# A causal convolution on TensorE: from two column tiles of 64 to four of 32

## The chip, the cores and the metric

The kernel runs on one core of a Trainium2 chip. A core has TensorE (PE: matmuls, and PEld for the weight loads that go with them), VectorE (DVE), ScalarE (ACT), GpSimd (POOL) and SyncE (SP), each with its own stream of instructions, and 16 DMA engines that they share. The metric is the device time of one execution in microseconds; a kernel's time is the median of several runs.

## The reference

The input x has 8 sequences of 3264 rows and 192 channels. A causal convolution of 7 taps comes first, with softmaxed weights of its own for each of 8 heads of 24 channels. Then a spectral mix: the lowest 64 modes of a Fourier transform along the sequence are multiplied by a complex 192 x 192 matrix for each mode, transformed back and added, and a channel matmul with ReLU is added to that.

```python
# convolution: H = 8 heads, K = 7 taps, group = D // H
w = softmax(weight)
out = np.einsum('hk,bskhg->bshg', w, x_unf)     # x_unf: the 7 rows up to s

# spectral mix of x = out
X = np.fft.rfft(x, axis=1)
Yr = einsum('bmd,mde->bme', Xr, w_r) - einsum('bmd,mde->bme', Xi, w_i)
Yi = einsum('bmd,mde->bme', Xr, w_i) + einsum('bmd,mde->bme', Xi, w_r)
Y[:, :n_modes] = Yr + 1j * Yi
y = np.fft.irfft(Y, n=S, axis=1)
u = x + y
return u + np.maximum(u @ w_ch, 0.0)
```

## The kernel before

The eight sequences are taken as four pairs (`q`), and each pair as 13 blocks (`t`) of 256 rows, the last of 192. A block is loaded as two halves of 128 rows, one row to a partition, into `xall`. Blocks are grouped into units: the first pair in four (2, 3, 4 and 4 blocks), the others in three (5, 4, 4), 13 units in all.

There are three stages, written in a fixed order of instructions (`manual_schedule`), which each engine keeps.

**Convolution and DFT.** `conv_group(k, g)` convolves unit `k` for two heads, so a unit has four groups. The convolution is a matmul with a band matrix made from the taps: `band[:, e, h, :]` gives, from 128 input rows, the outputs at even (`e = 0`) or odd (`e = 1`) rows. Output goes to PSUM, where partition p holds rows 2p and 2p + 1 of the block. L309 makes 64 output partitions from each half of 128 rows, on column tile 0 or 64 of the PE array. A few outputs need rows from the half before: L317 adds them for the upper 64 partitions, L314 for the lower ones from the block before, L321 for the first block of a unit, whose rows before are kept in `side` (L336). ACT (L328) or DVE (L330) then copies the group back over `xall`, as bf16, and three PSUM buffers `zc` go round. `dft_unit` (L344) sums the blocks' Fourier transforms with the table `ftab`, which DVE and ACT compute at the start (`table_dve`, `table_act`) from the row numbers `sidx` that a POOL iota made (L164).

**Weights.** PE transposes the table (`g_bank`, L421) and the convolved blocks (`ct_bank`, L431), and between these multiplies the modes by their matrices (`mix`, L471), four modes to a group, 16 groups. The matrices have seven slots; a slot's next load is issued after the mix that read it (`load_free`, L281).

**Output.** For each of 52 blocks 28 matmuls (L501), a ReLU on ACT (L528), an addition on DVE (`finish`, L536) and a store from SP (L540), into buffers that go round.

All loads of x and of the matrices are DMAs issued by POOL in program order. At the start these are units 0 to 3, a memset of the unused half of the last blocks (L252), the last blocks of all pairs (`load_last`, L155), then POOL's own small constants and units 4 on (L143), the small matrices, and the mode matrices (L281). L237 builds the band matrix: 152 matmuls of 8 columns on four column tiles of 32.

## Time and profile before

| what | value |
|---|---|
| median of 3 runs | 184.12 us (183.80 to 184.87) |
| the profiled execution, its own time | 183.47 us |
| its span in the profile | 181.7 us, mean granted PE clock 0.979 |
| instructions of the profile | 7678 |
| PE busy, weight loads busy | 165.1 us (91%), 140.1 us (77%) |
| DVE, ACT, POOL busy | 113.9 us (63%), 99.1 us (55%), 52.2 us (29%) |
| DMA | 40.27 MB moved, mean 222 GB/s |
| stores from SP | 52, one for each block, 372 ns median to issue, 3.7 us to landing |

The profile page has the busy time of each engine, the span in 40 equal slices of 4.54 us (each digit is a share in tenths), the DMA queues, the chain of work that ended last, and the costliest groups of instructions. In the chain a piece is a start, a length and what ran; "issue" is time in which the engine waited for nothing that the profile shows. In a timeline a row is a start, a length, engine, line, operation, output and inputs, and in brackets the idle time before it and what ended it. L-numbers are lines of the kernel.

### The profile page before, as it was taken

To read this page: it belongs to the slowest core of one execution; us is meant where nothing else is said; L and a number is where in the kernel's file an instruction comes from. 1 tells how busy PE (TensorE), PEld (TensorE's weight loads), DVE (VectorE), ACT (ScalarE), POOL (GpSimd) and SP (SyncE) were. 2 spreads that over 40 slices of the span, in tenths; PEclk is the share of its full clock that TensorE was granted. 3 is DMA by queue.
4 is the path that set the end of the run, shared out by engine and by line. 5 is a ranking of instruction groups with operands and counts; after the bars stand their busy time and mean duration, and the time that the engine had idled before them with its cause. 6 is when DMAs were issued, how large, how long until landed. Compare 5 with 4: busy or idle time off the path is not lost.

```text
span 181.7 us, 7678 instructions
## 1 busy us (share of the span) xinstructions
PE 165.1 (91%) x3440; PEld 140.1 (77%) x3440; DVE 113.9 (63%) x160; ACT 99.1 (55%) x138; POOL 52.2 (29%) x84
## 2 busy tenths in 40 slices
PE   7958799999999997999999985899999999999970
PEld 2437578888887885788997852499999999999960
DVE  3676944444544554577767600678888888888880
ACT  2442593353362452568777721666666666666750
POOL 7995694434322744055520220000000000000000
PEclk9996999999999999999999999999999999999995
DMA  2999999999999999999999394069998999999995
GB/s 24 159 166 190 191 192 195 189 193 192 191 192 193 205 206 207 206 192 190 201 207 207 59 174 79 4 236 338 345 316 318 361 330 349 341 323 330 351 352 171
DMA packets 49808, 40.27 MB, mean 222 GB/s; under 512 B 28399, under 2 KB 49775, under 8 KB 49775
## 3 DMA queue, kind: packets, MB, share of 16 engines
q0 software_dynamic: 35680, 19.69, 79.0%
q1 hardware_dynamic: 14095, 20.09, 31.5%
q8 instruction: 27, 0.44, 0.9%
q14 instruction: 6, 0.05, 0.1%
HBM read 39.40 MB, written 20.05 MB: 327 GB/s over the span
## 4 chain that ended last, share of the span: by engine, by line
PE 80%; DMA 6%; ACT 4%; issue 3%; DVE 3%; POOL 0%; DVEq 0%; ACTq 0%
PE z_right L501 17%; PE z_left L501 16%; PE w_left L431 10%; PE x_right L344 9%; PE x_left L309 8%; DMA arena<-in_moe_w_i_dram 4%; PE x_right L309 3%; PE w_right L471 3%; PE x_left L317 3%; PE x_left L314 2%; DMA ct<-in_weight_dram 2%; PE w_left L421 2%; PE x_right L317 2%; PE x_right L189 1%; ACT xall L328 1%
## 5 line engine op out<-in xcount | busy, mean ns | idle before, releaser
L501 PEld LDWEIGHTS <-gt 64*128 64x128 bf16 (+1 forms) x832 | 35.9, 96 | 1.7 <-issue 1.6
L309 PEld LDWEIGHTS <-bandyet 128*64 128x64 bf16 x416 | 32.2, 114 | 4.9 <-issue 4.1
L317 PE MATMUL x_left<-xall,bandyet 128*64 128x192 bf16 (+3 forms) x140 | 26.5, 254 | 3.9 <-issue 3.9
L330 DVE CAST xall<-x_left 128x768 bf16<-128x768 f32 (+3 forms) x18 | 16.8, 935 | 20.5 <-PE x_left L321 10.8
L309 PE MATMUL x_left<-xall,bandyet 128*64 128x192 bf16 (+3 forms) x280 | 27.9, 256 | 0.2 <-ACT xall L328 0.2
L501 PEld LDWEIGHTS <-ct 64*128 64x128 bf16 (+1 forms) x624 | 27.3, 96 | 0.5 <-issue 0.4
L143 POOL DMA_DIRECT2D xall<-in_x_dram x26 | 22.9, 884 | 14.9 <-DMA xall<-in_x_dram 13.8
L317 PEld LDWEIGHTS <-bandyet 128*64 128x64 bf16 x208 | 23.5, 114 | 4.3 <-issue 4.3
L314 PE MATMUL x_left<-xall,bandyet 128*64 128x144 bf16 (+3 forms) x140 | 25.8, 232 | 0.0
L528 ACT ACTIVATE z_right<-z_right 128x768 f32<-128x768 f32 (+1 forms) x26 | 20.7, 794 | 9.4 <-PE z_right L501 9.0
L528 ACT ACTIVATE z_left<-z_left 128x768 f32<-128x768 f32 (+1 forms) x26 | 20.7, 795 | 9.0 <-PE z_left L501 9.0
L501 PE MATMUL z_left<-fz,gt 64*128 64x192 bf16 (+1 forms) x416 | 24.7, 243 | 0.1
L501 PE MATMUL z_right<-fz,gt 64*128 64x192 bf16 (+1 forms) x416 | 24.2, 243 | 0.5 <-ACT z_right L528 0.5
L314 PEld LDWEIGHTS <-bandyet 128*64 128x64 bf16 x208 | 23.6, 116 | 0.0
L328 ACT CAST xall<-x_left 128x768 bf16<-128x768 f32 (+3 forms) x17 | 13.9, 816 | 14.5 <-DVE side L336 7.4
L409 DVE COPY ct<-w_left 128x1024 bf16<-128x1024 bf16 x24 | 15.9, 689 | 7.4 <-PE w_left L431 5.3
L344 PE MATMUL x_right<-xall,fz 128*128 128x384 bf16 (+1 forms) x104 | 19.2, 327 | 1.4 <-DVE xall L330 1.1
L431 PE MATMUL w_left<-ident,xall 128*128 128x128 bf16 x312 | 19.6, 220 | 0.0
L431 PEld LDWEIGHTS <-xall 128*128 128x128 bf16 x312 | 17.6, 103 | 1.8 <-issue 0.3
L501 PE MATMUL z_right<-wch,ct 64*128 64x192 bf16 (+1 forms) x312 | 17.5, 243 | 0.2 <-ACT fz L448 0.2
L501 PE MATMUL z_left<-wch,ct 64*128 64x192 bf16 (+1 forms) x312 | 17.5, 243 | 0.0
L407 ACT COPY ct<-w_left 128x1024 bf16<-128x1024 bf16 (+1 forms) x16 | 15.3, 960 | 3.7 <-PE w_left L431 3.4
(109 smaller groups left out, 292.0 us busy)
## 6 DMA issues: line engine op xcount, KB each, us to landing
out_dram<-arena SPq DMA_DIRECT2D x25, 384.0 KB, 3.7
out_dram<-xt SPq DMA_DIRECT2D x12, 384.0 KB, 3.8
out_dram<-ct SPq DMA_DIRECT2D x11, 384.0 KB, 3.5
xall<-in_x_dram POOLq DMA_DIRECT2D x8, 384.0 KB, 14.0
xall<-in_x_dram POOLq DMA_DIRECT2D x10, 288.0 KB, 12.8
xall<-in_x_dram POOLq DMA_DIRECT2D x6, 480.0 KB, 14.4
ct<-in_moe_w_r_dram POOLq DMA_DIRECT2D x8, 288.0 KB, 7.8
ct<-in_moe_w_i_dram POOLq DMA_DIRECT2D x8, 288.0 KB, 8.3
```

What stands on the lines that cost most here:

```text
L143: nc.gpsimd.dma_start(out=dst, in_=src)
L309: nc.tensor.matmul(cols[r, :, e, :].rearrange("p t (i d) -> p t i d", i=2), band[:, e, h, 0:64], xall[:, q, t0:t0 + n, half, :, dsl], star ...
L314: nc.tensor.matmul(cols[0:64, 1:n, e, :].rearrange("p t (i d) -> p t i d", i=2), band[:, e, h, 64:P], xall[:, q, t0:t0 + n - 1, 1, :, dsl] ...
L317: nc.tensor.matmul(cols[64:P, :, e, :].rearrange("p t (i d) -> p t i d", i=2), band[:, e, h, 64:P], xall[:, q, t0:t0 + n, 0, :, dsl], star ...
L328: nc.scalar.copy(out=dst, in_=srcv)
L330: nc.vector.tensor_copy(out=dst, in_=srcv)
L344: nc.tensor.matmul(xp, ftab[0:r, 2 * t + e, :], xall[0:r, q, t, e, :, :].rearrange("p i d -> p (i d)"), start=(t == 0 and e == 0), stop=(t ...
L407: nc.scalar.copy(out=out, in_=in_)
L409: nc.vector.tensor_copy(out=out, in_=in_)
L431: nc.tensor.transpose(tp[:, P * k:P * k + P], src, ident[:])
L501: nc.tensor.matmul(zt[0:l.shape[-1], i, D * e:D * e + D], l, r, start=begin, stop=end, tile_position=(64 * i, 0), skip_group_check=True)
L528: nc.scalar.activation(out=zt[0:m, :, 0:2 * D], in_=zt[0:m, :, 0:2 * D], func=ACT.Relu)
```

## The change

Three things are changed.

The convolution makes 32 output partitions at a time, on column tiles 0, 32, 64 and 96 (`tile_position=(0, 32 * ct_)`). Only the first 32 of each 64 outputs of a half need rows from the half before, so the matmuls for these ("spill") go to two of the four tiles. Even blocks (`t`) stand as before; odd blocks are stored 32 partitions on, so that their spill goes to the other two tiles. Even and odd blocks are separate matmuls, with every second block of the unit in the columns.

The row numbers in `sidx` follow the rotation, with three iotas, and a finished odd block is stored in two transfers: partitions 32 to 127, and partitions 0 to 31, which hold its last 64 rows.

On POOL's queue the memset of the unused half goes between the loads of the second and third unit, and the loads of the last blocks go ahead of those of the fourth.

```diff
-    nc.gpsimd.iota(sidx.rearrange("p (t e) -> p t e", e=2), pattern=[[256, NB], [1, 2]], base=0,
-                   channel_multiplier=2, allow_small_or_imprecise_dtypes=True)
+    s3 = sidx.rearrange("p (t e) -> p t e", e=2)
+    for t0, p0, p1, base in ((0, 0, P, 0), (1, 0, P, 256 - 64), (1, 0, 32, 256 + 192)):
+        nc.gpsimd.iota(s3[p0:p1, t0:NB:2, :], pattern=[[512, (NB + 1 - t0) // 2], [1, 2]], base=base,
+                       channel_multiplier=2, allow_small_or_imprecise_dtypes=True)
...
     load_unit(*units[1])
+    nc.gpsimd.memset(xall[64:P, :, NB - 1, 1, :, :], 0.0)
     load_unit(*units[2])
+    load_last(0)
+    load_last(1)
     load_unit(*units[3])
...
-    nc.gpsimd.memset(xall[64:P, :, NB - 1, 1, :, :], 0.0)
-    load_last(0)
-    load_last(1)
...
-        for hd in range(2):
+        def mm(hd, e, c, spill, odd):
             h = 2 * g + hd
             dsl = slice(GRP * h, GRP * h + GRP)
-            cols = zt[:, hd, 0:96 * n].rearrange("p (t e c) -> p t e c", t=n, e=2)
...
+            ct_ = (c + odd) % 4
+            t1 = t0 + (t0 + odd) % 2
+            out = zt[32 * ct_:32 * ct_ + 32, hd, 0:96 * n].rearrange("p (t e c) -> p t e c", t=n, e=2)
+            lhs = band[:, e, h, 64:96] if spill else band[:, e, h, 32 * (c % 2):32 * (c % 2) + 32]
+            first = e == 0 and odd == t0 % 2 and not spill
+            def one(ts, src):
+                o = out[:, ts[0] - t0:ts[-1] + 1 - t0:2, e, :].rearrange("p t (i d) -> p t i d", i=2)
+                nc.tensor.matmul(o, lhs, src, start=first, stop=False, tile_position=(0, 32 * ct_),
+                                 skip_group_check=True)
+            ts = list(range(t1, t0 + n, 2))
+            if spill and c == 0:
+                back = [t for t in ts if t > t0]
+                if back:
+                    one(back, xall[:, q, back[0] - 1:back[-1]:2, 1, :, dsl])
+                if ts[0] == t0 and t0:
+                    one(ts[:1], sd[:, :, dsl].unsqueeze(1))
+            else:
+                one(ts, xall[:, q, ts[0]:ts[-1] + 1:2, (c - spill) // 2, :, dsl])
+        w = t0 % 2
+        for hd in range(2):
             for e in range(2):
-                for half in range(2):
...
+                for c in range(4):
+                    mm(hd, e, c, 0, w)
+                mm(hd, e, 0, 1, w)
+                mm(hd, e, 2, 1, w)
+                for c, spill in ((0, 0), (2, 0), (0, 1), (2, 1), (1, 0), (3, 0)):
+                    mm(hd, e, c, spill, 1 - w)
...
-        dst = bass.AP(tensor=out.tensor, offset=out.offset + (2 * q * S + 256 * t) * D,
-                      ap=[[2 * D, m], [S * D, 2], [1, 2 * D]])
-        nc.sync.dma_start(out=dst, in_=o[0:m].rearrange("p i e d -> p i (e d)"))
+        for p0, p1, r0 in (((32, P, 0), (0, 32, 192)) if t % 2 else ((0, m, 0),)):
+            dst = bass.AP(tensor=out.tensor, offset=out.offset + (2 * q * S + 256 * t + r0) * D,
+                          ap=[[2 * D, p1 - p0], [S * D, 2], [1, 2 * D]])
+            nc.sync.dma_start(out=dst, in_=o[p0:p1].rearrange("p i e d -> p i (e d)"))
```

More of the change, by code (lines that the diff above doesn't have):

```diff
@@ L301, in conv_group @@
         sd = side[k % 2]
-        for hd in range(2):
+        def mm(hd, e, c, spill, odd):
             h = 2 * g + hd
             dsl = slice(GRP * h, GRP * h + GRP)
-            cols = zt[:, hd, 0:96 * n].rearrange("p (t e c) -> p t e c", t=n, e=2)
-            for e in range(2):
-                for half in range(2):
-                    r = slice(64 * half, 64 * half + 64)
-                    nc.tensor.matmul(cols[r, :, e, :].rearrange("p t (i d) -> p t i d", i=2),
-                                     band[:, e, h, 0:64], xall[:, q, t0:t0 + n, half, :, dsl],
-                                     start=(e == 0), stop=False, tile_position=(0, 64 * half),
-                                     skip_group_check=True)
-                if n > 1:
-                    nc.tensor.matmul(cols[0:64, 1:n, e, :].rearrange("p t (i d) -> p t i d", i=2),
-                                     band[:, e, h, 64:P], xall[:, q, t0:t0 + n - 1, 1, :, dsl],
-                                     start=False, stop=False, tile_position=(0, 0), skip_group_check=True)
-                nc.tensor.matmul(cols[64:P, :, e, :].rearrange("p t (i d) -> p t i d", i=2),
-                                 band[:, e, h, 64:P], xall[:, q, t0:t0 + n, 0, :, dsl],
-                                 start=False, stop=(t0 == 0), tile_position=(0, 64), skip_group_check=True)
-                if t0:
-                    nc.tensor.matmul(cols[0:64, 0, e, :].rearrange("p (i d) -> p i d", i=2),
-                                     band[:, e, h, 64:P], sd[:, :, dsl],
-                                     start=False, stop=True, tile_position=(0, 0), skip_group_check=True)
```

## The prediction

> **What bounds the kernel now.** I read the slices first, then the chain of waits, then the PE's timeline inside the convolution, and last the DMA queue that carries instructions.

> ```profile
> PE   7958799999999997999999985899999999999970
> PEclk9996999999999999999999999999999999999995
> DMA  2999999999999999999999394069998999999995
> ...
> q8 instruction: 27, 0.44, 0.9%
> ```

> The DMA engines are full from slice 1 on (4.5 us) to about 100 us, and the PE from slice 5 (about 23 us) on. The chain says which ends last:

> ```profile
> 71.45 0.97 DVE xall L330
> 72.46 1.48 PE x_right L344 x8
> 73.94 1.01 PE w_left L421 x32
> ...
> 104.79 0.60 POOL arena L281
> 105.39 6.60 DMA arena<-in_moe_w_i_dram
> 112.03 0.48 PE w_right L471 x12
> ```

> Convolution and DFT are a PE chain up to 73.9 us. The weight stage is a PE chain of 30.2 us up to the mix that frees the last slot (104.1), then a 6.6 us load. The output stage is PE again, 1.155 us a block. So a shift of the 73.9 moves the end one for one, until the loads themselves come last. The x loads (10.0 MB at 192 GB/s) are done near 58 us, the seven weight groups that have a free slot (4.1 MB at 206 GB/s) near 78.

> The PE's timeline holds the line that decides this case:

> ```profile
> 6.29 1.38 PE L237 MATMUL x_right<-ct 7*32 7x8 bf16 x152 [0.22 <-DVE ct L233]
> ...
> 11.29 0.19 PE L314 MATMUL x_left<-xall,bandyet 128*64 128x48 bf16 x1
> 14.30 0.29 PE L317 MATMUL x_left<-xall,bandyet 128*64 128x96 bf16 x1 [2.81 <-issue]
> ...
> 19.62 0.23 PE L314 MATMUL x_left<-xall,bandyet 128*64 128x144 bf16 x1
> 20.97 0.27 PE L317 MATMUL x_left<-xall,bandyet 128*64 128x192 bf16 x1 [1.12 <-issue]
> ```

> Twice the PE stops inside a conv group, between an L314 and an L317 that read data which is already there; "issue" means that the profile shows nothing it waited for. From 14.30 to the second stop, one window counts:

> ```profile
> 14.30:20.96 6.66, 5.37 (x127) 5.10 (x127) 5.71 (x8) 2.53 (x4) 3.63 (x5) 0.78 1.60 191
> 28.66:35.18 6.52, 6.52 (x135) 5.63 (x131) 3.34 (x4) 3.20 (x4) 3.31 (x4) 1.00 1.60 192
> 42.41:48.92 6.51, 6.51 (x133) 5.62 (x129) 3.10 (x4) 3.20 (x4) 2.74 (x4) 1.00 1.60 192
> ```

> **Matmuls (conv_group).** A group of four blocks now has five matmuls per head and parity, 768 columns in sum on two column tiles of 64: 4 x 768 / 2 columns; it takes 0.69 us (41.77 to 42.46). After the change it has 12 matmuls per head and parity, mostly of 96 columns, 13 where history comes from the side buffer: 4 x 1152 / 4, three quarters of the columns, if four tiles overlap as two do now: 0.52 us. Seven eighths of the convolution lies behind 26 us: 45 of 52 blocks, at 8.8 us per 13 blocks (four groups of 0.82, eight of 0.69), 30.5 us, of which a quarter is 7.6 us. That is the whole gain.

> No row shows 128 rows by 32 columns with 96 moving columns. Nearest is L237: 152 pairs on four tiles of 32 in 1.38 us, 9.1 ns a pair, here 10 ns from the columns. The other bound is that only two of four overlap: 20 ns, 1.04 us a group. I take 10 ns; both lie under the fetch, below.

> [...]

> **Instructions.** The order of instructions of the two programs has 976 conv matmuls before and 2,624 after, each with its weight load: 3,296 instructions more. Up to the first transpose of the weight stage (L421 now) it counts 2,569 before and 5,865 after. The stall at 14.30 is at row 446 of that order; it stays where it is, as the page asked for at 6.9 us does. Behind it stand (5865 - 446) / 255 = 21.2 pages (255: a semaphore wait each) instead of 8.3. A page's work is 128 pairs at 10 ns plus its share of the DFT (8 matmuls of 0.175 us to about 1.9 pages), some 2.1 us: less than any fetch above. So the PE starves:
> - 14.3 to 27.0 us: 2 pages (6.6, 6.1).
> - 27.0 to 58, x loads running: 31 / 5.15 = 6.0 pages.
> - 58 to 78, weight loads running: 20 / 4.75 = 4.2 pages.
> - then no data moves, since group 7 waits for the first mix: 9.0 pages x 2.9 = 26.1 us, to 104.1.
> - the last copy and DFT, 1.5 us of the 2.5 that the chain shows: 105.6.

> The weight stage starts at 105.6 instead of 73.9, 31.7 us later, and keeps its 38.1 us: its PE work asks for a page every 6.6 us, its loads again wait for the mixes. Sum on the profiled execution: 183.5 + 31.7 = 215.2 us. That run is 0.65 under the median of 184.12, inside the spread of the runs; I say 215.

> Bounds: pages of 4.4 us while data moves and 2.3 idle (no 0.5 of the tail, which both stalls have under load) give 11.6 + 2 pages by 78, 7.6 x 2.3 = 17.5, end near 97, 207 us. Pages of 5.5, and 3.9 idle (the slowest of the output stage) give 9.3 + 2, 9.9 x 3.9, end near 118, 228. A stalled PE also loses clock (0.60 in the window 14 to 18 us, after the first stall): at half clock a page's 2.1 us become 4.2, hidden under load, up to 1.3 a page over 2.9 without, 12 us at most.

> [...]

> **The rest is nothing, and what covers it.** Two more iotas (0.31 us each now) and the memset of 1.37 us go ahead of the third unit's loads on POOL; the loads issued by then are 0.96 MB, 5 to 6 us at 160 GB/s, which covers these 2 us. Without that cover x would come 2 us later, under a PE that is late anyway. The four DMAs of the last blocks (2.98 us of POOL) pass the two of the fourth unit: the same bytes in another order, for a unit that the PE reaches after 27 us. The iotas feed L200 at 6.16 us and end before 4. On SP, 24 blocks get a second store: an issue is 0.37 us, so 0.74 in a period of 1.155, no queue; uncovered it would be 24 x 0.37 = 9 us. Bytes and rows are the same; the last block keeps one transfer. DVE and ACT run as many instructions as before.

> **Rivals.**
> 1. Faster, 176 us: fetching keeps up and four tiles overlap. The 7.6 us come off; the last loads allow about that much (after 78 us, nine groups of 2.9 us end at 104.4 instead of 112.0). For it: 220 instructions per us ran at L237, and the burst needed no wait. Against: that burst came from what was loaded at the start, and the stall followed it. It decides if a page takes under 2.9 us while data moves. 7%.
> 2. Slower by little, 187 us: every page takes the 2.9 us that row 102.9 shows, the long ones being only late requests. 14.3 + 21.2 x 2.9 + 1.5 = 77.3, 3.4 us later. Against: 6.66 us between two stalls is no late request. 8%.
> 3. The fetch binds as above and the pair costs 20 ns or the clock halves in the idle stretch: 9 pages x 1.3 more, 227 us. 12%.
> That it does not do what it says: the order of instructions shows the 2,624 matmuls, so this falls away.

> **How the numbers follow.** Forecast 215 at 73%. The range reaches down to 200, between the second rival and the low bound of 207, and up to 226, just short of the third. About 0.5% is what a measurement of this kernel can tell from no change: faster 0.07, within it 0.01, slower 0.92.

> **What would show it.** The PE's waits name "issue" some twenty times, 2 to 5 us each in units of 256 instructions; q8 moves 40 packets, 0.65 MB; the first transpose starts near 105 us; the DMA row shows a hole between 78 and 105; PEclk falls below 9 in the convolution; a block of the output stage stays at 1.155 us. If q8's packets come less than 2.5 us apart while x loads run, my reading of one page at a time is wrong, and with it the forecast; if the convolution's pairs take over 40 ns without waits named "issue", the PE and not the fetch was the bound.

## The result, and the profile after

| what | before | after |
|---|---|---|
| median of 4 runs | 184.19 us (183.80 to 184.87) | 242.69 us (241.94 to 245.00) |
| the profiled execution's span | 181.7 us | 240.2 us |
| first transpose of the weight stage starts | 73.94 us | 122.07 us |
| last addition of the output stage starts | 176.48 us | 226.77 us |
| from there to the end of the span | 5.2 us | 13.4 us |

The change makes the kernel slower: ratio 1.319, 95% interval 1.309 to 1.330. The forecast was 215 us with a range of 200 to 226, so the direction was right and the size was not.

The span grew by 58.5 us, and three rows of the table say where: 48.1 us up to the first transpose, 2.2 us more up to the last addition (50.3 - 48.1), and 8.2 us behind it. The page after shows the first and the last of these in its slices of 6.0 us:

```profile
PE   7523365585564866969599999868999999999600
PEclk9955557587796799997979999999999999999975
DMA  5999999999999200000006999480899899899985
...
q8 instruction: 40, 0.66, 1.0%
```

Counted from 0, slices 1 to 19 show a PE that is busy about half of most of them. DMA stands nearly still from slice 14 to slice 20 (84 to 126 us), waiting for the first mix, and in the last two slices stores run while the PE has nothing left. The instruction queue moved 40 packets, as forecast. The chain of waits (start, length, what ran) shows what filled the first part:

```profile
12.96 0.47 PE x_left L318 x20
13.51 0.48 PE x_right L318 x26
13.99 0.60 PE x_left L318 x31
14.59 4.93 issue
19.52 0.84 PE x_left L318 x34
...
119.38 0.97 DVE xall L346
120.39 1.68 PE x_right L360 x8
122.07 1.85 PE w_left L437 x16
...
154.90 6.24 DMA arena<-in_moe_w_i_dram
...
226.77 0.95 DVE arena L552
```

A burst of convolution matmuls from 12.96 us, 1.63 us long, then 4.93 us in which nothing that the profile shows was waited for. The engine's waits, summed over 9 to 119 us (us in total, times, longest), name nothing else of that size on the PE. The two rows are largely the same stalls, seen by the weight loads and by the matmuls, and are not to be added:

```profile
PEld L318 <- issue: 50.4, 33, 5.1
...
PE x_left L318 <- issue: 35.9, 16, 4.9
```

The windows from one page boundary to the next (stretch, length, busy time and count of PE, weight loads, DVE, ACT, POOL, then granted clock, DMA share, GB/s) give the price of a page of 256 instructions:

```profile
12.96:19.53 6.57, 1.64 (x129) 1.50 (x129) 3.15 (x5) 1.22 (x2) 5.89 (x11) 0.50 1.59 191
25.72:32.07 6.35, 2.35 (x128) 2.13 (x128) 2.15 (x3) 3.12 (x4) 2.26 (x4) 0.50 1.60 192
50.84:57.04 6.20, 3.38 (x129) 2.44 (x129) 1.57 (x3) 1.44 (x2) 1.76 (x3) 0.97 1.60 192
88.56:92.29 3.73, 3.46 (x128) 2.45 (x128) 0.96 (x1) 1.32 (x2) 0.00 (x0) 1.00 0.02 4
99.31:103.13 3.82, 3.37 (x128) 2.40 (x128) 2.37 (x3) 1.44 (x2) 0.00 (x0) 1.00 0.02 4
```

A page is some 128 pairs of a weight load and its matmul. While x is loaded (192 GB/s) a page takes 6.1 to 6.6 us, whatever the PE's own part is, 1.64 or 3.38 us; beside the matrix loads after that it takes 5.9 to 6.0. With the data queues still it takes 3.4 to 3.9, but for one page (107.04 to 111.70 us) in which the PE itself was busy throughout, at a granted clock of 0.63. Eleven pages from 12.96 to 81.10 us take 6.19 us on average, the nine from 84.93 to 118.86 take 3.77. The queue itself shows one such page under load and one in the idle stretch, with the windows 50.84 to 57.04 and 99.31 to 103.13 cut into 40 slices of 155 and 95 ns:

```profile
GB/s 196 191 193 193 191 191 191 186 188 191 193 196 198 193 188 188 193 191 188 188 193 186 198 196 294 186 176 176 181 173 178 186 188 191 193 196 196 186 188 186
...
q8 instruction: 1, 0.02, 1.0%
...
GB/s 0 0 0 0 0 0 0 0 0 0 0 172 0 0 0 0 0 0 0 0 0 0 0 0 0 0 0 0 0 0 0 0 0 0 0 0 0 0 0 0
...
q8 instruction: 1, 0.02, 1.9%
```

In the idle page the packet starts 1.1 us after the page ahead was entered (slice 11; a packet's bytes are put down at its start). It takes 1.2 us (1.9% of 16 engines' 3.82 us), and the PE goes on 1.5 us after it ended. Under load (slice 24 of the first row) the same three parts are 3.9, 0.95 and 1.4 us: nearly the whole difference between 6.2 and 3.8 is the time until the packet starts.

### The profile page after: what moved, and what is told of

Read it like the earlier page. It is cut to its first block, busy times and chain, and to the rows that moved or that the text cites. A ratio compares the mean times of both kernels' runs of the same rounds, so it can differ in the third digit from the quotient of the medians.

```text
span 240.2 us, 11017 instructions
## 1 busy us (share of the span) xinstructions
PE 175.7 (73%) x5086; PEld 143.5 (60%) x5088; DVE 112.9 (47%) x160; ACT 99.6 (41%) x138; POOL 52.9 (22%) x86
## 4 chain that ended last, share of the span: by engine, by line
PE 64%; issue 18%; DMA 6%; DVE 4%; ACT 2%; SPq 0%; POOL 0%; DVEq 0%; ACTq 0%
PE x_left L318 12%; PE z_right L517 12%; PE x_right L360 10%; PE z_left L517 10%; PE w_left L447 8%; PE x_right L318 5%; DMA arena<-in_moe_w_i_dram 3%; PE w_right L487 2%; DMA out_dram<-arena 2%; PE w_left L437 2%; DMA ct<-in_weight_dram 2%; DVE arena L552 1%; PE w_right L500 1%; PE x_right L373 1%; PE w_left L455 1%
## 5 line engine op out<-in xcount | busy, mean ns | idle before, releaser
L318 PEld LDWEIGHTS <-bandyet 128*32 128x32 bf16 x2624 | 37.5, 108 | 52.2 <-issue 50.4
L318 PE MATMUL x_left<-xall,bandyet 128*32 128x96 bf16 (+2 forms) x1668 | 32.1, 228 | 32.1 <-issue 31.4
L344 ACT CAST xall<-x_left 128x768 bf16<-128x768 f32 (+3 forms) x17 | 13.9, 818 | 42.5 <-PE x_left L318 33.4
L360 PE MATMUL x_right<-xall,fz 128*128 128x384 bf16 (+1 forms) x104 | 25.6, 404 | 1.1 <-DVE xall L346 1.1
L344 ACT CAST xall<-x_right 128x768 bf16<-128x768 f32 (+1 forms) x9 | 6.9, 764 | 35.4 <-PE x_right L318 31.3
L318 PE MATMUL x_right<-xall,bandyet 128*32 128x96 bf16 (+2 forms) x812 | 16.0, 226 | 4.9 <-issue 4.9
L318 PE MATMUL x_left<-side,bandyet 128*32 128x48 bf16 x92 | 16.2, 197 | 4.5 <-issue 4.5
L284 POOL DMA_DIRECT2D ct<-in_moe_w_r_dram x8 | 5.0, 619 | 61.4 <-PE w_right L487 59.0
L346 DVE CAST xall<-x_right 128x768 bf16<-128x768 f32 (+2 forms) x8 | 8.1, 1008 | 21.5 <-PE x_right L318 21.3
L517 PE MATMUL z_left<-wch,ct 64*128 64x192 bf16 (+1 forms) x312 | 17.5, 243 | 0.0
```

Of the source, the lines that this page charges most:

```text
L284: nc.gpsimd.dma_start(out=slots[slot_of[g]][64 * half:64 * half + 64, :, :, :], in_=src[4 * g:4 * g + 4, :, :].rearrange("m (p j) e -> p m ...
L318: nc.tensor.matmul(o, lhs, src, start=first, stop=False, tile_position=(0, 32 * ct_), skip_group_check=True)
L344: nc.scalar.copy(out=dst, in_=srcv)
L346: nc.vector.tensor_copy(out=dst, in_=srcv)
L360: nc.tensor.matmul(xp, ftab[0:r, 2 * t + e, :], xall[0:r, q, t, e, :, :].rearrange("p i d -> p (i d)"), start=(t == 0 and e == 0), stop=(t ...
L517: nc.tensor.matmul(zt[0:l.shape[-1], i, D * e:D * e + D], l, r, start=begin, stop=end, tile_position=(64 * i, 0), skip_group_check=True)
```

## The experiments

**The stores, put back alone.** The changed kernel with one store for each block:

```diff
-        for p0, p1, r0 in (((32, P, 0), (0, 32, 192)) if t % 2 else ((0, m, 0),)):
...
+        dst = bass.AP(tensor=out.tensor, offset=out.offset + (2 * q * S + 256 * t) * D,
+                      ap=[[2 * D, m], [S * D, 2], [1, 2 * D]])
+        nc.sync.dma_start(out=dst, in_=o[0:m].rearrange("p i e d -> p i (e d)"))
```

> The changed kernel with one store for an odd block: the rows of odd blocks land rotated by 64 rows in the output, the bytes are the same. If the second store makes the output stage longer, as the 13 us between the last addition and the end suggest, the whole is near 233 us and that gap is back at 5 us. If the stores are not the cause, 242 us.

Measured 231.98 us, ratio 1.255 (1.237 to 1.274). The first transpose starts at 120.53 and the span is 229.4 us, 47.7 over before: without the second stores the kernel is late by the convolution and by little else. The medians differ by 10.7 us. But the profiles put 1.5 us of that ahead of the first transpose (122.07 against 120.53), where nothing is stored yet. From the start of the last addition to the end it is 5.8 us here, and 13.4 with the second stores. So the second stores are worth some 8 to 9 us: a term of the forecast that stood at nothing is about a seventh of the loss.

**The stores, added alone to the kernel before.** Odd blocks of the old kernel stored in two, cut in three ways: partitions 32 to 127 and 0 to 31 as in the change, two halves of 64 partitions, or all 128 partitions with one sequence each.

```diff
+        for p0, p1 in (((32, P), (0, 32)) if t % 2 else ((0, m),)):      # split
+        for p0, p1 in (((64, P), (0, 64)) if t % 2 else ((0, m),)):      # split64
+        for i0, i1 in (((0, 1), (1, 2)) if t % 2 else ((0, 2),)):        # splitseq
...
```

> The kernel before, with odd blocks stored in two transfers of 96 and 32 partitions, in place (no rotation). If the split alone makes the output stage longer: about 9 us more, 193 us. If it is hidden, as predicted: 184 us.

> The kernel before, with odd blocks stored in two transfers of all 128 partitions, one for each sequence: as many transfers as in the split by partitions. Theory that the number of transfers costs: the same 193 us. Theory that transfers of few partitions cost: 184 to 186 us.

> The kernel before, with odd blocks stored in two transfers of 64 partitions. Number of transfers: 193 us as for 96 and 32. Few partitions: between 184 and 193 us, or more than 193 if every transfer under 128 partitions is slow.

Measured: split 192.38 us, ratio 1.045 (1.038 to 1.052); split64 192.78, 1.048 (1.041 to 1.055); splitseq 184.34, 1.001 (0.997 to 1.005). All three issue 76 transfers instead of 52, of the same bytes in sum. So the number of transfers, and with it SP's 24 more issues, costs nothing that shows; a transfer over part of the partitions does. One window of 50 us in the output stage, of split and then of splitseq:

```profile
125.00:175.00 50.00, 49.34 (x1191) 48.87 (x1187) 39.99 (x43) 33.70 (x43) 0.00 (x0) 1.00 0.93 290
```

```profile
125.00:175.00 50.00, 50.00 (x1218) 50.00 (x1214) 41.46 (x44) 34.50 (x44) 0.00 (x0) 1.00 0.95 333
```

The DMA engines are as busy in both (0.93 and 0.95), but move 290 instead of 333 GB/s; before it was 338. The packets of the data are of 1,536 bytes in all of them, and in this window the slowest tenth take 112 ns or more in split, and 73 or more in splitseq and before. An issue on SP has a median of 616 ns in split, 388 in splitseq, 372 before. Whether the longer issues cost time of their own, or only wait for engines that are full, was not tried apart. In the changed kernel SP is behind from the middle of the stage on:

```profile
184.68 2.86 SPq L557 DMA_DIRECT2D out_dram<-arena  x3
187.62 2.73 SPq L557 DMA_DIRECT2D out_dram<-xt  x3
190.44 5.13 SPq L557 DMA_DIRECT2D out_dram<-arena  x6
```

Twelve issues, all but back to back, 0.86 to 0.95 us each on average in a row. The forecast had two of 0.37 us in a period of 1.155.

**When the matrices are loaded.** The changed kernel with the matrix loads held behind the last convolved block, by a small POOL copy that reads it. It tells whether the long page is bound to data moving.

```diff
     dft_unit(len(units) - 1)
+    nc.gpsimd.tensor_copy(out=ct[0:32, 3, 0:16], in_=xall[0:32, NQ - 1, NB - 1, 0, 0, D - 16:D])
     load_free(0)
```

> The changed kernel with the mode matrices' loads held back until the convolution is done, so that no data moves after the x loads end near 58 us. Theory that data traffic makes a page 6.2 instead of 3.6 us: 14 pages at 3.6 us from 58 us on, first transpose near 111 us instead of 122, then the matrices late, the whole near 240 us. Rival (a page's time has nothing to do with the data): first transpose at 122 us and the whole near 252 us.

Measured 244.06 us, ratio 1.321 (1.300 to 1.342). Two windows between page boundaries, one before the x loads end and one after:

```profile
43.98:56.48 12.50, 9.29 (x256) 6.13 (x256) 3.33 (x4) 2.24 (x3) 2.92 (x5) 0.75 1.60 192
70.96:107.37 36.41, 27.11 (x1278) 20.29 (x1277) 14.24 (x18) 11.97 (x16) 0.00 (x0) 1.00 0.02 5
```

Two pages take 12.5 us under load, 6.25 each; the ten from 70.96 us on take 36.41, 3.64 each, of which the PE is busy 2.71. The changed kernel was still at 6.0 a page there (69.17 to 75.18 to 81.10) in the same part of the program. So the loads set the longer price. The last copy of the convolution is done by 112.6, 7.7 us earlier than the changed kernel's at 120.35, and the matrices, now loaded behind it, take that back.

**Only the number of instructions, first attempt.** The kernel before, with 8 or 4 more tiny matmuls for each head and parity, into columns of PSUM that nobody reads (`shift`, 7 x 32, as in L237):

```diff
             for e in range(2):
+                for x in range(8):                                       # pad4: range(4)
+                    nc.tensor.matmul(xtrb[32 * (x % 4):32 * (x % 4) + 32, 500:508], shift[0:KK, 0:32], taps_t[0:KK, :],
+                                     start=True, stop=True, tile_position=(0, 32 * (x % 4)), skip_group_check=True)
                 for half in range(2):
```

> The kernel before with 1,664 more matmuls of 7 rows, 32 columns and 8 moving columns in the convolution, into columns that nobody reads: 5,897 PE instructions up to the first transpose, as many as in the changed kernel (5,865), with the old column tiles, the old columns and the old single stores. Fetch theory (a page of 256 instructions at a time, 6.2 us while loads run, 3.6 us after): the first transpose near 122 us, as in the changed kernel, the whole near 233 us. Rival (the matmuls themselves, or the narrow tiles, cost the time): 1,664 x 9.1 ns = 15 us, the whole near 199 us.

> The same with 832 more matmuls, 4,233 instructions up to the first transpose, 14.9 pages after the first stall. Fetch theory: 10.6 pages of 6.2 us up to 80, 4.3 of 3.6 us, first transpose near 97 us, the whole near 207 us. Rival: 832 x 9.1 ns = 7.6 us, the whole near 192 us.

Both missed: 269.53 and 271.11 us for 1,664 and 832 more matmuls, or 267.4 and 267.7 in the faster run of each (185.28 before). Half the additions cost the same, so this measured something else than a count. The PE's timeline of the kernel with eight, and the windows of two rounds:

```profile
40.41 0.22 PE L308 MATMUL x_right<-ct 7*32 7x8 bf16 x8
40.56 0.37 PE L312 MATMUL x_right<-xall,bandyet 128*64 128x192 bf16 x2
40.72 0.33 PE L317 MATMUL x_right<-xall,bandyet 128*64 128x144 bf16 x1
...
41.02 0.22 PE L308 MATMUL x_right<-ct 7*32 7x8 bf16 x8
...
40.41:41.02 0.61, 0.61 (x16) 0.47 (x14) 0.00 (x0) 0.61 (x2) 0.61 (x1) 0.50 1.61 193
143.22:143.64 0.42, 0.42 (x16) 0.33 (x13) 0.00 (x0) 0.00 (x0) 0.00 (x0) 1.00 0.00 0
```

A round of 13 matmuls takes 0.61 us (40.41 to 41.02) at a granted clock of 0.50, and 0.42 at 1.00; with four pads it takes 0.58 and 0.40. Before, five took 0.17 at 1.00 (the group of four rounds in 0.69). So part of the loss is a lower clock, 0.83 on average with eight pads and 0.78 with four, and part is there at full clock. The pads alternate small weights on four tiles with large ones on two; whether the tile's width, its rows or the order is to blame was not tried apart. This pair says nothing for or against the fetch, and the pads had to be of the old form.

**Only the number of instructions, in the old form.** Pads with the convolution's own weights and column tiles of 64, 8 columns wide. In pad8w they read `xall`; in pad8x and pad4x (4 instead of 8) the zeros of `blank`, which nothing writes in that stage.

```diff
             for e in range(2):
+                for x in range(8):
+                    p0 = 64 * (x % 2)
+                    nc.tensor.matmul(xtrb[p0:p0 + 64, 500:508], band[:, e, h, 0:64], blank[:, 0:8],
+                                     start=True, stop=True, tile_position=(0, p0), skip_group_check=True)
```

> As pad8, but the 1,664 added matmuls have the shape of the convolution's own: 128 rows, 64 columns on tile 0 or 64, 8 moving columns, so that the array keeps one division. 5,898 instructions up to the first transpose. Fetch theory: pages of 6.2 us until the loads pause near 80 us, then 3.6 to 4, first transpose 119 to 125 us, the whole 230 to 236 us, with waits named issue at every 256 instructions. Rival (what pad8 and pad4 showed is a cost of any added matmul, whatever its shape): as pad8, 269 us, and no such waits.

> As pad8w, but the added matmuls read zeros that nothing overwrites, so that they wait for no copy. Fetch theory: pages of 6.2 us up to about 82 us (row 3,521), then 9.4 pages of 3.6 to 4.0 us (the PE's own work is 3.9), first transpose near 121 us, the whole near 231 us. Rival (the added matmuls' own 16 ns each, as pad8w shows it in the stretch without stalls): 1,664 x 16 ns = 26 us, the whole near 210 us.

> As pad8x with 832 added matmuls, 4,234 instructions up to the first transpose. Fetch theory: 11 pages of 6.2 us to 82 us, then 3.9 pages of 4.3 us (the PE's own work), first transpose near 100 us, the whole near 210 us. Rival: 832 x 16 ns = 13 us, the whole near 197 us.

Measured: pad8w 254.47 us, ratio 1.388 (1.366 to 1.409); pad8x 244.15, 1.328 (1.318 to 1.338); pad4x 216.66, 1.179 (1.170 to 1.188). In pad8w the pads read columns that ACT overwrites, so they wait for copies (0.89 us for `ACT xall L332` before the pads at 95.30 us), a fault of the experiment. Pad8x is the clean one. Its total of 5,897 instructions before the first transpose is that of the changed kernel (5,865) within 0.6%, with the old tiles and stores:

```profile
19.85:26.15 6.30, 4.05 (x128) 3.96 (x127) 4.43 (x6) 1.28 (x2) 5.23 (x8) 0.57 1.60 192
```

A page is 6.30 us here as well. It enters its pages at 13.66, 19.85, 26.15 ... 74.98 and 81.17 us; the changed kernel does at 12.96, 19.53, 25.72 ... 75.18 and 81.10. Twelve boundaries agree within 0.7 us in two programs that share the count and not the tiles. That shows the fetch as the bound while the loads run. Behind 82 us pad8x goes its own way: 4.9 us a page (ten from 81.17 to 130.39 us), with waits of the pads (L309) for the DVE and ACT copies out of `xtrb`, the tile that the pads write (rows of the whole run),

```profile
PE x_right L309 <- issue: 10.1, 6, 2.3
PE x_right L309 <- DVE xt L369: 4.8, 3, 1.6
PE x_right L309 <- ACT xt L371: 3.3, 3, 1.1
```

so its 244 us, 13 over what the fetch theory gave, must not be read as the fetch's price for the whole; the first 80 us are. Pad4x keeps 6.2 us up to 82 us too, is limited by the PE behind it, and ends 7 us over the theory's 210.

**Four tiles without the rotation.** Four column tiles of 32, even and odd blocks in one matmul and one store each: 1,392 convolution matmuls instead of 976 or 2,624. The spill then lies on two tiles only. `one` is a matmul of 32 output partitions on tile 32 * c.

```diff
+                for c in range(4):
+                    one(c, e, False, 0, n, xall[:, q, t0:t0 + n, c // 2, :, dsl])
                 if n > 1:
...
+                    one(0, e, True, 1, n, xall[:, q, t0:t0 + n - 1, 1, :, dsl])
...
+                one(2, e, True, 0, n, xall[:, q, t0:t0 + n, 0, :, dsl])
                 if t0:
...
+                    one(0, e, True, 0, 1, sd[:, :, dsl].unsqueeze(1))
```

> The convolution on four column tiles of 32 without the rotation: even and odd blocks in one matmul of up to 240 columns, spill on tiles 0 and 64, one store for each block. 1,392 conv matmuls, 3,401 instructions up to the first transpose, 11.6 pages after the first stall. Fetch theory: 6.2 us a page up to 80 us, the last page 5.2 (its own work), first transpose near 86 us, the whole near 196 us. Rival (each narrow matmul costs what it cost in the changed kernel, 108 us / 2,624 = 41 ns): 1,392 x 41 ns = 57 us, convolution done near 67 us, the whole near 178 us.

Measured 198.88 us, ratio 1.084 (1.072 to 1.097). Its pages are entered every 5.9 to 6.5 us from 14.83 to 77.08. From its 3,401 instructions and 6.2 us a page, the fetch theory gave 196 before the run; a price of 41 ns for each narrow matmul, the rival, gave 178.

| kernel | instructions to first transpose | first transpose |
|---|---|---|
| before | 2,569 | 73.94 us |
| norot | 3,401 | 88.07 us |
| pad4x | 4,233 | 105.67 us |
| after | 5,865 | 122.07 us |
| pad8x | 5,897 | 134.02 us |

**Fewer instructions and a shorter weight stage.** If instructions are scarce, fewer should help: lean makes the band matrix with 38 matmuls instead of 152. Fill holds ten transposes of the weight stage back for the stretch in which the PE waits for the last matrices; filllean does both.

```diff
-        for g in range(4):
-            nc.tensor.matmul(xtrb[32 * g:32 * g + 32, H * i:H * i + H],
...
+        nc.tensor.matmul(xtrb[0:32, H * i:H * i + H],
...
```

> The kernel before, with the band matrix made by 38 matmuls instead of 152: 228 PE instructions less, all ahead of the first stall. Fetch theory: the two stalls of 2.8 and 1.1 us move and shrink, the convolution ends 1 to 3 us earlier, 181 to 183 us. Rival (the first 26 us are set by the table on DVE and ACT): 184 us.

> The kernel before, with the ten transposes of the last pair (5.6 us of PE) held back until after the mixes: mix 11 and 12 come earlier, so the last two groups of matrices are asked for near 97 us instead of 103, and the transposes fill the wait. Theory that the weight stage ends with the loads: they end near 105 us instead of 112, the whole near 178 us. Rival (the loads come no sooner, or the mixes then wait for their matrices): 184 us.

> fill and lean together. If lean's 1 us at the end of the convolution is worth anything behind fill: 177 us; if the loads are then the bound: as fill.

Lean: 183.23 us, ratio 0.996 (0.992 to 1.001), not told from no change. The two stalls at page boundaries are gone (the first boundary is now crossed at 17.42 us without a wait) and the first transpose comes at 72.88 instead of 73.94, but the PE then waits for x instead. Fill: 185.29, 1.011 (1.001 to 1.021); filllean: 185.83, 1.014 (1.005 to 1.023), both missed the 177 to 178 expected. Fill's chain shows why:

```profile
91.62 11.17 DMA arena<-in_moe_w_i_dram
...
104.41 4.37 PE w_left L431 x78
...
111.14 0.97 PE w_right L189 x4
...
112.49 1.83 PE w_right L189 x8
```

The loads do end earlier, at 108.2 us instead of 111.7. But ten transposes are more than the wait had room for, and 12 matmuls of L189, whose results nobody uses and which stood in that wait before, now stand in the way, 2.8 us of them.

**The version that beats both.** Five transposes held back, and the 12 idle matmuls left out:

```diff
+    last = [tjobs.pop() for _ in range(5)][::-1]
     for d in range(ND - 1):
         mix(2 * d)
-        some(3)
+        some(2)
         mix(2 * d + 1)
         mix_copy(d)
-        some(5)
+        some(4)
         mix_trans(d)
...
-    assert not tjobs
+    tjobs += last
+    some(len(tjobs))
...
-    active(4, yps[0], ident[:], gt[:, 0, 0:4, :])
     mix(2 * d)
-    active(8, yps[0], ident[:], gt[:, 0, 0:4, :])
     mix(2 * d + 1)
```

> As fill, with five transposes held back instead of ten and without the twelve idle matmuls between the last mixes: in fill the loads did end at 107 us, but the PE still had transposes and idle matmuls to run until 114 us. If that was all, the last mix is near 109 us and the whole 181 us. Rival (without the idle matmuls the clock drops, or the mixes still wait): 184 us or more.

Measured 181.01 us (180.76 to 182.10), ratio 0.986 (0.979 to 0.993). A load on its chain, the held transposes, the last mix and the start of the output stage:

```profile
91.99 11.18 DMA arena<-in_moe_w_i_dram
...
105.34 2.14 PE w_left L431 x38
...
109.85 0.67 PE w_right L471 x20
...
115.26 1.00 PE z_right L501 x20
```

The last matrices land at 108.8 us instead of 111.7, and the output stage's `z_right` row starts at 115.26 us, where it started at 117.38 before. The gain has nothing to do with the change under study; it comes from the wait that the prediction's chain showed at 105.39 us. What each of the two edits is worth was not tried apart.

## Why the prediction was wrong

**Right: the bound.** The PE starves for pages of 256 instructions that come one at a time: both windows that are cut into slices above hold one packet, and each of the 40 is of 16,384 bytes in the trace, the prediction's 64 for each of 256 instructions. That a page is asked for when the PE enters the page before it was my reading: the trace has a packet's start and length, and no row shows a request. The matmuls' waits name "issue" 21 times between 9 and 119 us, in units of 256 instructions, the queue moved 40 packets, and the same count in old tiles (pad8x) gives the same boundaries. Pairs stood 10 to 14 ns apart inside the bursts at a granted clock of 1.00, nearer the prediction's estimate of 10 for four tiles at work together than its 20 for two, and 11 to 18 at 0.50 (one burst 26); no pair came near the 40 ns that would have made the PE the bound. The first rival (176 us) and the second (187) fall: no page of the starved stretches takes as little as 2.9 us, loaded or not. The third rival's 227 us is nearer in number and not in cause: the clock fell to 0.50 in early pages, under cover of the fetch, and was 0.95 on average in the idle stretch where the rival needed it low; only the one page of 4.66 us is of its kind. The weight stage all but kept its length (first transpose to end of the last load: 38.1 us before, 39.1 after), and nothing in the trace points to the POOL reorder or the iotas, which no run tried apart.

**Wrong, the larger part: "For later pages, which came in time, I add the 1.5 us to the packet's end".** This gave 6.1, 5.15, 4.75 and 2.9 us; the runs show 6.19 on average under load (5.9 to 6.6) and 3.77 without. The same sum with the measured prices, from the same 14.3 us: (78 - 14.3) / 6.19 = 10.3 pages, then 10.9 x 3.77 = 41.1, and 1.5, together 120.6 us instead of 105.6. The trace has 122.07. A page's own work was mis-sized too, 2.1 us against 2.86 measured from 81.10 to 118.86 us, but all but one page hid it under the fetch.

Why were the later pages' prices too short? I measured each from the moment in which the PE executed the first instruction of the page ahead. Where the PE is far from starved, the trace shows packets that start before that moment: in the changed kernel one 0.6 us before it (152.93 against 153.53 us), and in pad4x one 1.1 us before (93.11 against 94.24). An estimate from the packets of the kernel before: counted from the instruction 48 places earlier, the four between 28 and 57 us start after 3.75 us, with a scatter of 0.06 instead of 0.42 us, beside 3.8 to 4.2 where the changed kernel is starved. The 48 are fitted to these four, not read from a row, and the next packet, at 58.12 us, comes out at 4.1. Which event a packet's start follows was not shown; what the runs show is that the prices of pages that came in time were too short. The one page that was entered straight from a stall (14.30 to 20.96 us), 6.66 us, had the price; I used it for one page, 6.1 us for the next and shorter ones for some nineteen. The premise that the fetch was "covered by about 2 us" was as wrong: by 6.2 us against pages of 6.5 to 7.2 the old convolution has 0.3 to 1.0 us to spare.

**Wrong, the smaller part: "The rest is nothing".** The second stores were counted as issues, 0.74 us in a period of 1.155, and found covered. The count was right and harmless, as splitseq shows. What was missed is that these transfers over part of the partitions move slower (290 and 297 GB/s in the windows of split and split64 against 333 in splitseq's) and take longer to issue (a median of 616 ns in split against 388): 8.3 us in the old kernel (192.38 - 184.1), some 8 to 9 in the new. Why they are slower, no row shows. The uncovered bound of 9 us, 24 x 0.37, is near in number by chance; it stood for 24 issues of unchanged length, and what changed is the DMA engines' rate and the length of an issue. So the sign "a block stays at 1.155 us" failed where the output buffers ran out (the store of 198.85 us in the chain holds the addition at 203.62), and the stores ran on to 13.4 us after the start of the last addition.

## What to carry to other kernels

Count instructions as you count bytes: before a matmul is split into smaller ones for the sake of the array, multiply the pages of the new count by the price of a page, and take that price from a stall in which the engine starved, never from a page that came in time. Here it was 6.2 us for 256 instructions beside the loads, 48 ns for a weight load and its matmul, and shorter pairs than that bought nothing. A store that was cut in two cost nothing here as long as both parts kept all 128 partitions (splitseq, ratio 1.001).

## What the runs showed of the hardware

- Instruction packets started later beside loads: a starved PE's packet started 3.8 to 4.2 us after the page ahead was entered while loads ran at 192 GB/s, and 0.9 to 1.2 us after with the data queues still. It is 16,384 bytes either way, and takes 0.9 to 1.3 us. Not all traffic showed this: in the old kernel's output stage, beside stores at 337 GB/s, ten packets started 0.2 to 1.4 us after the PE executed the first instruction of the page ahead (122.23 to 169.59 us). That PE was not starved, so these are no prices of a starved one.
- Splitting every second store by partition lowered the rate from 338 to 290 GB/s and raised an issue on SP from 0.37 to 0.62 us in the median. Splitting by sequence did neither by much (333 GB/s, 0.39 us). Why an issue gets longer was not tried.
- Alternating small matmuls on four tiles with larger ones on two cost 0.40 (four small ones) and 0.42 us (eight) a round at a granted clock of 1.00, and 0.58 and 0.61 at 0.50, where the five larger ones alone took 0.17 at 1.00.
- A clock of 0.50 in stretches where the PE is starved cost nothing that the page boundaries show: 6.35 us at clock 0.50 and 6.20 at 0.97. It did cost time where the fetch no longer covered it: the first 37 matmuls of the weight stage took 1.85 us at 0.50, where 38 took 1.01 at 1.00 in the kernel before.
- Still open: whether the fetch can be made to start sooner, and whether the rotation could pay with about as many instructions as before. Neither was tried.
